# One core, convolution beside windowed attention: the positions of the convolution kernel laid out in three channel groups instead of two halves, with a new order of the first list

## The chip, the cores and the metric

The kernel runs on one core of one Trainium2 chip. The metric is the device time of one execution in microseconds (us). The kernel before was run three times: 361.35, 356.34 and 360.53 us, median 360.53. One execution was recorded by the hardware profiler; it took 360.97 us, and 359.0 us lie between its first and its last instruction (the span). Times in views of the profile count from the first instruction.

The engines are named as the profile names them: PE is TensorE, DVE is VectorE, ACT is ScalarE, POOL is GpSimd, SP is SyncE, which issues most of the DMA transfers; POOL issues the others.

## The reference

An input x of 2048 positions and 640 channels goes through two branches, and a gate mixes them. Branch A is attention with 32 heads over a window of eight positions with a step of two. Branch B is a long convolution of each channel: its kernel K is a sum over 192 complex exponentials, and the convolution is done by a Fourier transform of twice the length.

```python
g = _sigmoid((x * gate_w).sum(-1, keepdims=True))
a = _A_ref(x, A_wqkv, A_wo)
b = _B_ref(x, B_A_re, B_A_im, B_B_re, B_B_im, B_C_re, B_C_im, B_log_dt, B_Dskip)
return g * a + (1 - g) * b
...
P = jnp.exp(logdA[:, :, None] * l[None, None, :])
K = jnp.einsum("dn,dnl,dn->dl", Cc, P, dB).real
...
y = irfft2(Uf * Kf) + u * Dskip
```

## The kernel before

The work is written as tasks. A task has a name, an engine (or a choice of ACT and DVE) and a function that issues its instructions. Two lists of tasks are issued one after the other, each in an order written out by hand: SEQ1 for the first list (L62 on), SEQ2 for the second. In SEQ1 a number stands for a task in the order in which tasks are declared, and a letter A or D after it chooses the engine where there is a choice. Each engine runs its own tasks strictly in this order, so a task that waits holds up everything behind it on its engine; the waits between engines follow from the data and from buffers. Costs and due times that stand beside the tasks have no effect once the order is written out.

The first list holds:

- The parameters of the convolution kernel (names such as rs8, mk9, sp9): computed on DVE and ACT, stored to DRAM in twelve pieces (Sprm), and loaded as L tiles (L00, L01 and so on).
- The attention: transposes of x (turn, tev) into xT, projections (late, evicted by lev), products of queries and keys (prod on DVE, summed on PE by lg), softmax (max, neg, exp, sum, at), the weighted values (pv on DVE, gat on PE, oT) and the output product (wo on PE, ga on ACT or DVE). ast and asb send the weights through DRAM; vc loads a window of values.
- The kernel K in ten chunks of 8 x 2 channels for each of four groups of partitions: args on PE (arg), sines and exponentials on ACT (act), products on DVE (pq, three for each chunk), sums on PE (kmm), and an eviction (fin) into the tile E. A task of chunk c has c behind its letters: act90000 is the first sine of chunk 9.
- The expansion of K, twice, for five chunks each (a half): shift, own and other on DVE and move and near beside them lay out the tile X; xst stores X to DRAM (Kx) and xld loads it back in another order as the tile kc. X and kc are made with one tag, xkc, in a pool of one buffer, so the next X is written only when the last reader of the kc before it is done.
- The first step of the Fourier transform: f1 (ten transforms from the first half's kc), fk (ten from the second half's) and fu (twenty from the input, Usb, loaded by rows0 to rows7). Each is eight small matmuls on PE into one of two "ar" buffers and one cast of 128 x 1024 on ACT or DVE (f1e, fke, fue) into bufA or big. own of the second half is declared to come after the last f1.

The sines and exponentials live in rings in the tile big; a fifth slot for sines lies in bufA at column NXT = 10240, over xT, which is free by then. fu writes into big, and every fu comes after all pq.

The second list is the rest of the Fourier transform, the product with the transformed kernel, the transform back and the mixing. It starts when the first list's casts are done. Its order isn't touched.

Here own begins, with X in the shared buffer, and the load of kc takes the same tag:

```python
x = X["X"] = pool["kk"].tile([128, 8, 9, CH], BF16, name="X", tag="xkc")
...
half[hf, "kc"] = now["kk"].tile([128, 64, CH], BF16, name="kc", tag="xkc")
```

Of the kernel before, what the change touches and what calls it, by code (L numbers as in the profile page):

```python
# [11 lines left out]
ALU = mybir.AluOpType  # L12
AX = mybir.AxisListType
F32 = mybir.dt.float32
BF16 = mybir.dt.bfloat16
# [47 lines left out]
0 2 3 1 6 8 4 14 13 26 5 7 27 9 10D 11D 12 18 74 76 28 75A 77A 78 79A 82 80 83D 15 17 23 81A 114 115D 120 94 56 121D 19 20 21 88 116 95A 89A 117A 37 100 92 104 101A 29  # L63
105A 93A 22 24 34D 35D 31 36 39 42 108 109A 25 86 118 106 90 119A 102 107A 32 103A 87A 110 96 84 16 38 30 111A 135 45 97A 40 33 46 41 136A 98 99A 43 44 229 51D 52 47 53
60 62D 122 146 85A 123A 57 147A 91A 125 129 230 126A 61 63 112 48 130A 113A 50 231 59 64A 152 154 153A 65A 155A 67 139 222 232 66 233 49 58 69 54 140A 68 70 55 71 72 234
127 137 73 235 128A 236 143 237 138A 223 144A 516 238 133 265 239 131 134D 240 148 267 224 132A 241 242 150 225 149A 151A 226 243 266 269 517 244 563 562 245 518 520 268
141 270 519 521 271 522 524 272 523 273 994 124 221 145 228 264 156 525 274 526 528 167 275 301 168D 142A 527 529 276 530 532 531 533 178 534 536 180 535 537 179A 303 538
540 539 541 175 181D 246 176D 186 542 544 277 278 543 545 187A 279 182 546 548 302 304 157 554 305 307 547 183A 549 158A 159 184 160A 306 308 550 552 551 553 185D 309 337
173 280 609 281 608 227 177 188 310 564 566 171 311 174A 565 312 567 313 172A 161 314 568 570 162A 569 571 556 315 339 165 572 574 338 573 575 166D 341 555 340 576 577
578 342 169 343 345 579 170A 163 580 582 199 581 583 584 586 585 587 557 344 346 558 588 590 589 591 200A 249 164D 559 347 600 373 203 592 594 593 204A 595 348 210 211A  # L70
205 560 596 598 206D 375 561 349 597 207 208D 350 201 351 189 602 599 202A 190A 610 612 611 613 601 374 376 377 614 616 247 615 617 379 618 620 191 248A 619 621 622 624
378 380 197 623 192A 625 626 628 252 381 605 409 198A 627 629 603 604 630 631 632 606 633 634 635 382 636 216 212 411 383 607 637 213D 646 316 655 352 654 317 638 217A
639 640 384 250 642 641 385 251A 643 644 645 214 386 656 648 387 195 215A 657 658 660 647 253 410 412 196A 659 661 254A 701 700 388 662 664 663 665 193 194A 282 651 413
666 667 668 255 257 670 256D 218 669 671 672 673 649 674 675 285 258D 415 219D 676 677 650 678 679 414 680 681 682 259 683 684 686 685 687 652 688 689 692 417 416 209 300
690 418 702 691 703 704 261 705 260A 706 708 283 707 709 710 653 694 445 419 262A 288 711 712 693 714 713 715 284D 447 697 716 718 717 719 695 720 721 722 420 724 723 725
755 756 263 353 726 727 286 289 728 729 730 696 732 731 733 734 698 421 735 318 287D 290D 738 699 736 291 737 757 758 759 760 739 761 762 422 763 765 764 766 740 423 743
292D 741 767 768 801 802 769 446 448 742 771 293 770 773 772 775 774 776 777 744 778 294A 779 781 295 780 782 783 784 449 321 745 793 451 795 746 785 787 786 789 297 788
296A 790 791 803 792 804 805 450 806 807 794 809 808 811 298A 810 812 319 813 453 320A 814 815 796 816 817 818 452 819 820 821 454 823 822 824 825 826 798 749 324 455 481
827 828 322 456 829 797 830 831 832 457 325 747 748A 833 458 834 835 799 836 837 323D 483 839 326A 750 459 800 424 847 848 299 389 751 894 893 460 220 336 372 752 849 327
838 850 851 482 852 841 485 853 484 854 855 840 857 856 858 859 486 861 860 487 328D 489 862 842 863 329 331 865 844 330D 864 866 867 869 488 868 871 870 873 843 872 874  # L80
875 877 333 876 878 879 881 880 882 845 354 332D 885 846 887 883 884 895 897 490 896 899 898 901 886 900 903 902 905 355 334A 904 906 491 357 360 356D 890 907 908 909 910
753 940 335 939 425 888 911 912 913 915 914 916 492 917 918 919 920 358 361 921 889 923 922 359D 362D 390 924 925 891 927 926 929 363 928 930 941 942 943 365 931 364D 892
366D 933 945 944 946 932 947 367 949 948 493 368D 950 951 952 369 953 391 955 393 934 392D 396 936 954 956 370A 935 494 957 371 754 995 996 997 408 998 999 1000 444 1001
# [79 lines left out]
class Attn:  # L163
# [20 lines left out]
    def window(self, pl, cst, pa):  # L184
# [8 lines left out]
        for n in range(2 * NKT):  # L193
# [8 lines left out]
            def ev(en, hf=hf, kt=kt, b=b):  # L202
                evict(nc, en, self.xT[:, hf, kt, :], b["tx"][:].rearrange("p a b -> p (a b)"))
# [4 lines left out]
    def plan_gate(self, pl, cst, pa, g_sb, late):  # L208
# [3 lines left out]
        def logit(_):  # L212
            b["gz"] = gz = pa.tile([128, 2, 512], F32, name="ar")
            for i in range(16):
                for kt in range(NKT):
                    nc.tensor.matmul(gz[:, 0, i:i + 1], self.xT[:, i // 8, kt, (i % 8) * 128:(i % 8 + 1) * 128], self.gw[:, kt:kt + 1], start=(kt == 0), stop=(kt == NKT - 1))
# [1095 lines left out]
```

## Time and profile before

| | before |
|---|---|
| median of 3 runs | 360.53 us (356.34 to 361.35) |
| profiled execution | 360.97 us |
| its span | 359.0 us |
| mean granted PE clock | 0.961 |
| first list ends, second begins | 283.3 us |
| busy, share of the span | DVE 87%, ACT 84%, PE 82%, POOL 22% |

A line of the groups names the line of code, the engine and the operation, then the tile written and the tiles read (numbers of buffers left out), the shape, the count, and behind the bar the busy time in us and the mean of one in ns. A line of a timeline begins with the start and the duration in us; rows of equal instructions that follow each other are merged (x8), and in brackets stand the idle time of the engine before it and what ended that. SPq and POOLq are issue slots, not transfers. Casts that go through the helper `evict` carry its line (L470 on ACT, L472 on DVE); there the tile names tell which task it is. bp is the result of f1, fk and fu, tb that of projections and output products.

### The profile page before, as it was taken

What the parts mean: (1) busy time and instruction counts of PE and PEld (TensorE: products, weight loads), DVE (VectorE), ACT (ScalarE), POOL (GpSimd) and SP (SyncE); (2) the same over time, 40 slices, a digit from 0 to 9 for tenths busy, and PEclk for the clock granted to TensorE, in tenths of its full rate; (3) what the DMA queues carried; (4) which work ended last, traced back from release to release, by engine and by line L of the source; (5) the groups of instructions that cost most, each with busy time, mean ns of one, the idle gap of its engine ahead of it and who ended that gap; (6) DMA issues with size and microseconds to landing.
All of it is one profiled execution on the core that took longest, in us unless ns stands there. A gap on an engine that the chain in (4) does not pass through costs nothing. (4 is left out here: it accounts for less than half of the span.)

```text
span 359.0 us, 12203 instructions
## 1 busy us (share of the span) xinstructions
PE 293.7 (82%) x5271; PEld 173.4 (48%) x5286; DVE 311.5 (87%) x413; ACT 303.0 (84%) x417; POOL 78.3 (22%) x125
## 2 busy tenths in 40 slices
PE   0199999699999999888887869999997799978760
PEld 0065564234544545445443424566664556647650
DVE  2899999669999899999998987999993479999982
ACT  1699997578989999999997979999895599888881
POOL 8930090211020100100012122416010023310032
PEclk9999999989999999999998978999998899999995
DMA  7951289421501611461256867489653149943047
GB/s 259 370 175 57 82 213 268 120 66 19 150 11 27 122 40 19 140 129 30 71 109 192 190 152 137 95 177 256 172 153 101 38 126 225 228 95 75 4 98 199
DMA packets 44042, 46.60 MB, mean 130 GB/s; under 512 B 24517, under 2 KB 38133, under 8 KB 43733
## 3 DMA queue, kind: packets, MB, share of 16 engines
q1 hardware_dynamic: 36116, 24.43, 26.2%
q0 software_dynamic: 5840, 20.55, 22.5%
q10 hardware_dynamic: 2032, 0.85, 0.9%
q8 instruction: 41, 0.67, 0.8%
q14 instruction: 13, 0.10, 0.1%
HBM read 31.31 MB, written 14.51 MB: 128 GB/s over the span
## 5 line engine op out<-in xcount | busy, mean ns | idle before, releaser
L291 PE MATMUL tb<-bufA 128*128 128x512 bf16 x285 | 71.7, 387 | 2.8 <-issue 1.1
L748 PE MATMUL ar<-Rarg,L 64*128 64x304 bf16 (+1 forms) x480 | 55.3, 282 | 14.7 <-ACT big L760 5.9
L760 ACT ACTIVATE big<-ar 128x608 bf16<-128x608 int16 x96 | 59.0, 681 | 8.2 <-PE ar L748 5.7
L762 ACT ACTIVATE big<-ar 128x864 bf16<-128x864 f32 x60 | 50.3, 917 | 3.6 <-PE ar L748 3.3
L291 PEld LDWEIGHTS <-bufA 128*128 128x128 bf16 x300 | 33.2, 120 | 31.7 <-issue 9.3
L420 DVE TENSOR_TENSOR pv<-vc,asb 128x4096 bf16<-128x4096 bf16 (+1 forms) x24 | 46.3, 1928 | 1.4 <-PE tb L426 1.4
L748 PEld LDWEIGHTS <-L 64*128 64x128 bf16 x480 | 21.4, 94 | 48.8 <-issue 41.9
L1009 PEld LDWEIGHTS <-PHI 128*128 128x128 bf16 x288 | 26.8, 99 | 18.0 <-issue 8.4
L801 PE MATMUL kps<-qq,pt 128*32 128x22 bf16 (+1 forms) x2560 | 26.3, 175 | 4.2 <-issue 4.2
L444 PE MATMUL tb<-wo_sb,oT 128*128 128x320 bf16 x160 | 28.1, 311 | 0.0
L801 PEld LDWEIGHTS <-pt 128*32 128x32 bf16 (+1 forms) x2560 | 22.5, 91 | 11.6 <-issue 8.7
L351 DVE TENSOR_TENSOR prod<-qk 128x2048 bf16<-128x2048 bf16 x20 | 24.1, 1220 | 2.9 <-PE lg L357 2.8
L351 DVE TENSOR_TENSOR prod<-prj 128x2048 bf16<-128x2048 bf16 x20 | 24.0, 1219 | 0.6 <-PE lg L357 0.5
L345 POOL DMA_DIRECT2D vc<-vS x16 | 11.5, 725 | 57.1 <-DVE pv L420 54.0
L426 PE MATMUL tb<-pv,ind 128*64 128x512 bf16 (+1 forms) x192 | 22.4, 361 | 0.2
L785 DVE TENSOR_TENSOR qq<-big 128x1408 bf16<-128x1408 bf16 x24 | 21.2, 885 | 0.0
L470 ACT ACTIVATE bufA<-bp 128x1024 bf16<-128x1024 f32 x16 | 16.0, 1032 | 5.6 <-PE bp L1232 5.5
L1009 PE MATMUL fp<-big,PHI 128*128 128x320 bf16 x112 | 17.9, 304 | 3.0 <-ACT sp_u L470 3.0
L200 PE MATMUL ar<-ident,xn 128*128 128x128 bf16 x80 | 8.1, 263 | 15.0 <-DMA xn<-in_A_x_dram 14.3
L470 ACT ACTIVATE sp_u<-fp 128x1280 bf16<-128x1280 f32 x14 | 17.3, 1237 | 3.4 <-PE fp L1009 3.4
L470 ACT ACTIVATE prj<-tb 128x512 bf16<-128x512 f32 x28 | 17.1, 612 | 3.1 <-PE tb L291 3.0
L470 ACT ACTIVATE big<-bp 128x1024 bf16<-128x1024 f32 x19 | 18.6, 1023 | 1.0 <-PE bp L1232 0.8
(173 smaller groups left out, 587.2 us busy)
## 6 DMA issues: line engine op xcount, KB each, us to landing
vc<-vS POOLq DMA_DIRECT2D x16, 327.5 KB, 6.9
PHI<-c_phi POOLq DMA_DIRECT2D x8, 384.0 KB, 4.9
Sprm<-pc SPq DMA_DIRECT2D x12, 240.0 KB, 2.0
L<-Sprm SPq DMA_DIRECT2D x80, 36.0 KB, 2.6
xn<-in_A_x_dram SPq DMA_DIRECT2D x4, 640.0 KB
gaS<-ga SPq DMA_DIRECT2D x8, 320.0 KB, 3.0
Usb<-in_A_x_dram POOLq DMA_DIRECT2D x8, 320.0 KB, 5.0
gaF<-gaS SPq DMA_DIRECT2D x8, 320.0 KB, 7.3
```

The lines of the kernel that those rows point to most:

```text
L291: nc.tensor.matmul(ppf, self.wq[:, kt, which * D + e:(which + 1) * D:5], self.xT[:, c0 // 1024, kt, c0 % 1024:c0 % 1024 + SC], start=(kt = ...
L351: nc.vector.tensor_tensor(b[e][:], self.part(ch, 0)[:, e, o:o + C].unsqueeze(1).to_broadcast([128, W, C]), win(self.part(ch, 1)[:, e, :], ...
L420: nc.vector.tensor_tensor(b["pv", e][:, 0:2 * n], taps, aw, ALU.mult)
L426: nc.tensor.matmul(b["op", e][64 * a:64 * a + 64, 0:n, :], self.twin, b["pv", e][:, a:2 * n:2, w, :], start=(w == 0), stop=(w == HV - 1), ...
L444: nc.tensor.matmul(apf[:, :320], b["oT"][:, e, i * 128:(i + 1) * 128], wo_sb[:, e, hf * 320:(hf + 1) * 320], start=(e == 0), stop=(e == 4))
L470: nc.scalar.activation(o, i, ACT.Identity)
L748: nc.tensor.matmul(ar[:, g2, a0:a0 + ncol], L[rows, sb, gp, l0:l0 + 128], R[rows, c0:c0 + ncol], start=True, stop=True, tile_position=(64 ...
L760: nc.scalar.activation(dst[:, 2 * gp:2 * gp + 2, sub, :], ar[:].bitcast(I16)[:, :, 0:2 * SW:2], ACT.Sin, scale=SCL)
L762: nc.scalar.activation(dst[:, 2 * gp:2 * gp + 2].rearrange("p g s n -> p g (s n)"), ar[:, :, 0:2 * EW], ACT.Exp)
L785: nc.vector.tensor_tensor(qq[:], trg[:, :, KI:].rearrange("p a (v m) -> p a v m", v=2), exq[:, :, KI:].unsqueeze(2).to_broadcast([128, 32, ...
L801: nc.tensor.matmul(kps[32 * g:32 * g + 32, h, NM * ql:NM * ql + NM], pt[rows, k, v, :], qq[rows, k, v, :], start=(g not in started), stop= ...
L1009: nc.tensor.matmul(o.rearrange("p (c x) -> p c x", x=32), phis[fb][:, fl, kind, :], B[:, :, 2 * f1 + ri].rearrange("p c q g -> p c (q g)") ...
```

## The change

The ten chunks are expanded in three groups, of four, four and two chunks, instead of two halves of five. E, nxt, X and kc are made at the size of the largest group and used up to the width of the group at hand; there are three DRAM tensors Kx instead of one, and three times shift, move, near, own, other, xst and xld. f1 has sixteen transforms (f10 to f115, for groups 0 and 1) and fk four (fk16 to fk19, for group 2). own of a group comes after the transforms of the group before it.

The two halves of xT change places in bufA, and the ring's fifth sine slot moves to column 16384. A transform of the input (fu) now comes only after those pq that read the part of the ring that it overwrites, instead of after all pq. SEQ1 is a new order throughout, including the choice of ACT or DVE for many evictions. The Dskip values are loaded by twelve small DMAs instead of eight.

```diff
-NXT = 10240
+NXT = 16384
...
-HC = NCH // 2
-CH = 2 * HC * CQ
+GRP = ((0, 4), (4, 8), (8, 10))
+GC = 2 * CQ * max(b - a for a, b in GRP)
...
-        self.Kx = dr.tile([2, 8, 4, KI, 8 * CH], BF16, name="Kx")
-
-    def expand(self, hf, E, pool, psp, S12):
+        self.Kx = [dr.tile([8, 4, KI, 8 * 2 * CQ * (b - a)], BF16, name=f"Kx{a}") for a, b in GRP]
+
+    def expand(self, gi, E, pool, psp, S12):
...
+        g0, g1 = GRP[gi]
+        CH = 2 * CQ * (g1 - g0)
...
-            x = X["X"] = pool["kk"].tile([128, 8, 9, CH], BF16, name="X", tag="xkc")
+            x = X["X"] = pool["kk"].tile([128, 72 * GC], BF16, name="X", tag="xkc")[:, 0:72 * CH].rearrange("p (h s c) -> p h s c", h=8, s=9)
...
-            f = pl.add(f"fin{c}", "D", 0.46, fn, deps=[m] + ([half["cp"]] if c == HC else []), after=fins[-1:], rel=[("kb", m0)], due=due)
-            if cl == HC - 1:
-                expand(hf, f, due + (pr["xl"] if hf == 0 else -50.0))
+            f = pl.add(f"fin{c}", "D", 0.46, fn, deps=[m] + ([half["cp", gi - 1]] if c == g0 and gi else []), after=fins[-1:], rel=[("kb", m0)], due=due)
+            if c == g1 - 1:
+                expand(gi, f, due)
...
-            if name == "f1":
-                half["own"].after.append(m)
+            if gi is not None and gi + 1 < len(GRP):
+                half["own", gi + 1].after.append(m)
...
-        for n in range(2 * HC):
-            first("f1", lambda: half[0, "kc"], Bk, n, half[0, "ld"] + [cst], xdone, pr["f0"] + pr["f1"] * n)
+        for gi, (a, b) in enumerate(GRP):
+            for n in range(2 * (b - a)):
+                first("f1" if b < NCH else "fk", lambda gi=gi: half[gi, "kc"], Bk, n, half[gi, "ld"] + [cst], (kg.pqs if b == NCH else []) + xdone, pr["f0"] + pr["f1"] * n, c0=a, gi=gi)
...
         for n in range(2 * NCH):
-            first("fu", lambda: P["Usb"], None, n, ub + [cst], kg.pqs, pr["u0"] + pr["u1"] * n)
...
+            lo = 2048 * (n // 2)
+            first("fu", lambda: P["Usb"][:], None, n, ub + [cst], [kg.pqs[k] for a, b, k in ends if a < lo + 2048 and b > lo], pr["u0"] + pr["u1"] * n)
```

The stretch of the new order around own1 (own of group 1), by engine, from act90000 on:

```
ACT  act90000 act90001 act90010 act90011 act90100 f1e0 near1 act90101 act90110 act90111 oT44 act90200 act90201 ga400 act90210
     f1e3 f1e7 f1e4 ga401 f1e6 f1e5 ga410 f1e1 ga411 f1e2 act90211 oT50 fue1 fue2 oT54
PE   arg90000 kmm800 arg90001 gat40 gat42 arg90010 arg90011 kmm810 arg90100 f10 sum7 move1 arg90101 arg90110 kmm811 arg90111
     gat44 arg90200 arg90201 wo400 arg90210 f13 wo401 f17 f14 kmm820 f16 wo410 f15 wo411 f11 f12 gat50 kmm900 arg90211 gat52 fu1 fu0
DVE  pq81 oT40 pv44 pq82 oT42 own1 other1 pv50 pq90 fin8 pv52 pq91 pv54 at7 fue0 oT52 f1e12 pq92 pv60 ga500 ga501 pv62 ga510
     ga511 fin9 shift2 own2 oT60 pv64 other2 pv70 ga600 ga601 fue19 ga610 pv72 pv74 fue8 fke17 fke16 ga710 fke19 fke18
SP   xst1S xld1S gaS4 ast7 asb7 gaS5 xst2S xld2S gaS6 gaS7
POOL rows0 xld0G rows1 rows2 rows3 vc1280 rows4 rows5 vc1536 rows6 xst1G rows7 xld1G vc1792 xst2G phi2 gates2 gates0 gates3 phi0 xld2G
```

In the order before, own1 (of the second half) stands after fin9, and all ten f1 stand ahead of it between chunk 9's args and kmm911; ahead of xst0 on POOL stand vc0 and vc256 next to each other right after halo1, where the new order has vc0, lst12, gst, halo2, vc256.

More of the change, by code (lines that the diff above doesn't have):

```diff
@@ L841, in near @@
         def near(en):
[L842 removed]
+            nxt = X["nxt"] = pool["kk"].tile([128, 7 * GC], BF16, name="nxt")[:, 0:7 * CH].rearrange("p (m c) -> p m c", m=7)
             for pt, (b0, n) in enumerate(((0, 4), (4, 3))):
@@ L1165, in gated_mix_kernel @@
     at.window(pl, acst, pa)
-    Dk = keep.tile([128, 2, CH], BF16, name="Dk")
+    Dk = keep.tile([128, 2 * CQ * NCH], BF16, name="Dk")
     nc.gpsimd.memset(Dk[:], 0.0)
@@ L1205, in fetch @@
                 for g in (0, 1) if e == "S" else (2, 3):
-                    kx.load(hf, half[hf, "kc"], g, nc.sync if e == "S" else nc.gpsimd)
-            half[hf, "ld"] = [pl.add(f"xld{hf}{e}", e, d, fetch, deps=st, due=due, dma=1.7) for e, d in (("S", 1.4), ("G", 1.1))]
+                    kx.load(gi, half[gi, "kc"], g, nc.sync if e == "S" else nc.gpsimd)
+            half[gi, "ld"] = [pl.add(f"xld{gi}{e}", e, d, fetch, deps=st, due=due, dma=1.7 * n / 5) for e, d in (("S", 1.4), ("G", 1.1))]
```

127 lines of the change are left out of this document (63 added, 64 removed).

## The prediction

> **What bounds the kernel now.** I read the page first (parts 1 and 2), then the table of windows, then the timelines of the windows where an engine stands idle, and the groups of instructions for durations.
>
> ```profile
> span 359.0 us, 12203 instructions
> PE 293.7 (82%) x5271; PEld 173.4 (48%) x5286; DVE 311.5 (87%) x413; ACT 303.0 (84%) x417; POOL 78.3 (22%) x125
> ACT  1699997578989999999997979999895599888881
> ```
>
> ```profile
> core 0: us, PE busy (x) PEld busy (x) DVE busy (x) ACT busy (x) POOL busy (x), PEclk, DMA share, GB/s
> 200.00:220.00 20.00, 16.02 (x415) 7.49 (x414) 16.04 (x22) 16.58 (x27) 4.38 (x8) 0.83 0.79 174
> 220.00:240.00 20.00, 18.94 (x494) 11.05 (x497) 19.96 (x28) 19.84 (x30) 5.96 (x8) 1.00 0.61 129
> 240.00:257.00 17.00, 15.80 (x428) 11.47 (x421) 16.98 (x26) 15.81 (x20) 6.16 (x11) 1.00 0.75 187
> 257.00:283.30 26.30, 21.88 (x264) 14.47 (x261) 18.50 (x23) 20.32 (x24) 1.78 (x3) 0.93 0.40 130
> ```
>
> VectorE (DVE) and ScalarE (ACT) bound the first list together: from 220 to 257 DVE is idle for 0.06 us and ACT for 1.35. Whatever holds either of them there is paid in full. The one large hole is the end of the list, 257 to 283.3, where DVE is idle for 7.8 us and ACT for 6.0. The timelines say why:
>
> ```profile
> 253.84 0.52 DVE L1215 CAST E<-kps 128x352 bf16<-128x352 f32 x1
> 255.41 1.66 DVE L847 COPY X<-E 128x640 bf16<-128x640 bf16 x8
> 256.99 0.73 DVE L847 COPY X<-nxt 128x80 bf16<-128x80 bf16 x3
> 257.34 0.37 SPq L875 DMA_DIRECT2D Kx<-X  x1
> 264.07 1.45 SPq L881 DMA_DIRECT2D kc<-Kx  x2
> 272.78 1.24 PE L1232 MATMUL bp<-F1c,kc 64*128 64x128 bf16 x16 [2.37 <-DMA kc<-Kx]
> 274.06 1.22 DVE L472 CAST bufA<-bp 128x1024 bf16<-128x1024 f32 x1 [3.18 <-PE bp L1232]
> 281.84 1.23 DVE L472 CAST bufA<-bp 128x1024 bf16<-128x1024 f32 x1 [0.56 <-PE bp L1232]
> 283.30 2.03 PE L1009 MATMUL fp<-bufA,PHI 128*128 128x320 bf16 x7 [1.11 <-ACT bufA L470]
> ```
>
> After the last kernel chunk (fin9, 253.84) its half is laid out (own1, other1), stored to DRAM (issued at 257.34, landed by 264.07: 6.7 us), loaded back (264.07 to 272.78: 8.7 us), and then ten transforms and casts follow until the second list starts at 283.30. The second list is the same in both kernels; it keeps its 75.7 us (283.30 to 359.0). So the forecast is the place of that start.
>
> **The end of the list, by itself: a gain.** The last group has two chunks where the last half had five. The round trip took 15.4 us; of that I keep two fixed parts of 2.6 us (the median landing of the 36 KB loads below) and scale the other 10.2 by 2/5: 5.2 + 4.1 = 9.3 us, between 6.2 (all of it scales) and 15.4 (none does). Four casts instead of ten follow it.
>
> ```profile
> L<-Sprm SPq DMA_DIRECT2D x80, 36.0 KB, 2.6
> ```
>
> Alone, this would let DVE run through. Counted task by task, its list up to fin9 is about 3 us longer in the new order (work that moved ahead), so fin9 ends at 257.5, and 17.5 us of DVE work (shift2 to fke18, with the durations of the part after next) plus some 2 of waits would end the list near 277: 6 us less.
>
> **The new wait: own1.** X and kc share one buffer (tag xkc, one slot). The new order expands group 1 while group 0's columns still stand in that buffer, so own1 waits until all eight f1 transforms of group 0 have been read out of it. In the order of each engine own1 is the next DVE task after pq82 and oT42, while the eighth transform, f12, comes on PE behind arg90210, f13, f17, f14, f16, f15 and f11. Each transform needs one of two "ar" buffers, so f12 starts when ACT has done f1e5. That point is counted on ACT's list:
>
> ```profile
> 229.78 1.25 ACT L760 ACTIVATE big<-ar 128x608 bf16<-128x608 int16 x2
> 234.03 0.45 ACT L470 ACTIVATE oT<-tb 128x256 bf16<-128x256 f32 x1
> 235.49 0.55 ACT L453 ACTIVATE ga<-tb,g_sb 128x320 bf16<-128x320 f32 x1
> 240.13 4.89 ACT L470 ACTIVATE bufA<-bp 128x1024 bf16<-128x1024 f32 x5
> 255.59 0.71 ACT L470 ACTIVATE nxt<-nxp 128x320 bf16<-128x320 f32 x2
> 242.11 0.46 PE L1232 MATMUL bp<-F1c,kc 64*128 64x128 bf16 x8 [0.23 <-ACT bufA L470]
> ```
>
> From act90000 to f1e5 the new list has 11 sines of 0.60, six casts of 0.95, near1 (0.65), oT44 (0.38) and two ga (0.45): 6.6 + 5.7 + 0.65 + 0.38 + 0.9 = 14.2 us. (A record overlaps the next by about 0.08 us, so I take distances between starts: two sines make 1.25, five casts 4.89.) act90000 started at 229.78. Ahead of it the new list gives ACT three more oT and one more ga, one lev less and near0 less: +0.6. Against this stands a start that may be earlier:
>
> ```profile
> 22.61 33.77 SPq L614 DMA_DIRECT2D Sprm<-pc  x12
> 50.28 2.86 POOL L345 DMA_DIRECT2D vc<-vS  x4
> 63.78 4.23 SPq L721 DMA_DIRECT2D L<-Sprm  x8
> 65.66 0.77 PE L748 MATMUL ar<-Rarg,L 64*128 64x304 bf16 x4 [1.69 <-DMA L<-Sprm]
> 44.49 0.85 POOL L317 DMA_DIRECT2D vS<-pv  x1 [21.99 <-ACT pv L470]
> ```
>
> The last parameter store was issued by 56.4 and the loads that need it only at 63.78, with four window loads (vc0, vc256) in flight from 50.28; the new order puts vc256 behind lst12 and gst. PE's wait of 1.69 bounds the gain, zero is the other end; I take 1.5, since half of the competing bytes go. So act90000 starts at 228.9, f1e5 ends at 243.1, and with 0.46 for f12 own1 starts at **243.5**.
>
> DVE is there long before:
>
> ```profile
> 231.22 0.69 DVE L783 TENSOR_TENSOR pt<-big 128x1024 bf16<-128x1024 bf16 x1
> 231.82 0.69 DVE L784 TENSOR_TENSOR pt<-big 128x1024 bf16<-128x1024 bf16 x1
> 232.42 0.89 DVE L785 TENSOR_TENSOR qq<-big 128x1408 bf16<-128x1408 bf16 x1
> 233.22 0.55 DVE L391 RECIPROCAL rs<-lg 128x64 f32<-128x64 f32 x1
> 233.81 0.69 DVE L392 TENSOR_TENSOR at<-at,rs 128x512 bf16<-128x512 bf16 x1
> ```
>
> These are pq82 and at7 of before. DVE's work up to pq82 is 1 us shorter in the new order, but gat40 and gat42 are later on PE, so oT42 ends between 233 and 236: a hole of 8 to 10.5 us. Queued behind own1 on DVE are other1, pv50, pq90, fin8; for these wait gat50 and kmm900 on PE, next in PE's order after f12, and behind them arg90211 and so ACT, which has only f1e1, ga411 and f1e2 (2.4 us) until then. So ACT doesn't use the hole either.
>
> **What is left after own1.** Counted on the new DVE list from own1 on, with these durations less 0.08 each:
>
> ```profile
> L420 DVE TENSOR_TENSOR pv<-vc,asb 128x4096 bf16<-128x4096 bf16 x16 | 36.5, 2282 | 0.3 <-PE tb L426 0.3
> L455 DVE TENSOR_SCALAR ga<-tb,g_sb 128x320 bf16<-128x320 f32 x20 | 10.8, 546 | 1.9 <-PE tb L444 1.9
> L420 DVE TENSOR_TENSOR pv<-vc,asb 128x2048 bf16<-128x2048 bf16 x8 | 9.7, 1218 | 1.1 <-PE tb L426 1.1
> L472 DVE CAST oT<-tb 128x512 bf16<-128x512 f32 x10 | 6.9, 686 | 2.9 <-PE tb L426 2.7
> ```
>
> Six large pv at 2.20 (13.2), three small at 1.14 (3.4), three pq at 2.00 (6.0), eight casts of transforms at 1.15 (9.2), eight ga at 0.47 (3.7), two oT (1.2), two fin (0.9), at7 (1.2), own1 and other1 (2.0: 2.4 at width 80, 1.9 if it scales to 64), shift2, own2 and other2 (1.5: between 1.0 scaled and 2.6): 42.3 us. As a check, the kernel before had 32.0 us of DVE work left at 243.5 (13.5 of the window to 257, and 18.50). Waits: 1 us at f1e12 (group 1's columns come about 14 us after other1, at own1 + 16, and f112 is wanted at 15); 2.5 in the last four casts, which alternate with the last output products (the last seven DVE tasks of before held 3.0 us of waits from 274.06 to 283.07); 0.5 elsewhere; together 4, between 1.5 and 6. Group 2 isn't late: other2 ends at own1 + 28.6, its columns come at + 37.9, and DVE reaches them at about + 38.5. End of the list: 243.5 + 42.3 + 4 = 289.8, 6.5 us after 283.3.
>
> [...] PE stands behind own1 until pv50 is done (own1, other1, pv50: 4.2 us), an idle stretch that before does not have there. The trace has such a case: after the 2.37 us in front of 272.78 the granted clock was 0.50.
>
> ```profile
> 273.00:274.00 1.00, 1.00 (x17) 0.82 (x17) 0.00 (x0) 0.37 (x1) 0.00 (x0) 0.50 0.08 18
> ```
>
> [...]
>
> From the trace alone, a half clock in the 4 us after own1 costs between 0 (DVE has pq90 and pv52 to do) and 2; I take 0.5. The sum is then 360.97 (the profiled execution, 1.97 above its span) + 7.0 = **368.0**. The three runs have a median of 360.53, 0.4 less.
>
> **What costs nothing.** The number of casts stays 40. The halves of xT change places together with the ring's fifth sine slot, whose first writer waits for the same 30 projections. Four more tiny Dskip loads take 2 us of POOL ahead of 44.49, where it idles for 21.99. xld0 on POOL now waits behind rows0 for prod74, which belongs to the time of chunk 6, and f10 wants its columns only in that of chunk 9. ast7 and asb7 stand on SP behind xld1, which waits until about own1 + 8, but at7 is only done at + 13; vc1792 on POOL likewise; pv70 wants both at + 28.6. Starting the input's transform by region gives nothing here, as fu1 stands behind gat52, about own1 + 10 = 253.5; in the kernel before it began at 248.4.
>
> ```profile
> 248.37 1.20 PE L1232 MATMUL bp<-F1c,Usb 64*128 64x128 bf16 x16
> ```
>
> **The rivals.**
> - *The wait is covered* (other side). It decides if f12 is read by the time DVE arrives, about 235; for that ACT must be 8 us ahead of my count. Its idle time between 200 and 220 (3.4) and PE's 1.69 speak for some of it, its full slices before that against. Then the end gains 6: 355; with the 1.5 us of the start 353. Chance 0.12, of it 0.08 faster by over 2%.
> - *Half the hole*: ACT 4 to 5 us earlier, own1 at 239: 363. 0.13.
> - *The hole grows*: half clock paid in full (1.7), asb7 or group 1's columns late (2), ACT without the early start (1.5): 373. 0.25.
> - *The forecast*: 365 to 371. 0.50.
>
> **How the numbers follow.** Two per cent, about what a measurement of this kernel can tell from no change, is 7.2 us: 353.3 and 367.7. Of the forecast's 0.50 I put 0.35 above that line. Slower 0.35 + 0.25 = 0.60; within 0.15 + 0.13 + 0.04 = 0.32; faster 0.08. The range of 8 in 10 leaves out the first rival and the far end of the third: 361 to 375.
>
> **What would show it.** Right: a DVE gap of 8 to 11 us ahead of the first X<-E copy of group 1, released by PE, starting near 234; an ACT gap of some 5 us shortly after; the second list's first product near 290; the last kc load within 6 us of its issue. Wrong: that gap under 4 us; own1 before 239; or a hole in another place, such as DVE waiting for parameters or for asb7.

## The result, and the profile after

The changed kernel took 371.94 us (median of four runs, 369.55 to 374.65) against 360.73 for the kernel before (four runs on the same chip, 356.34 to 361.35): the ratio is 1.034, 95% interval 1.023 to 1.045, slower. The profiled execution took 372.19 us. The prediction was 368.0, with a range of 361 to 375.

The first lines of its page, as those shown of before: the span, the busy times and ACT's 40 slices. ACT drops to 6, 2 and 5 tenths in the 27th to 29th slice (240.8 to 268.5 us).

```profile
span 370.4 us, 12252 instructions
...
PE 294.9 (80%) x5274; PEld 173.3 (47%) x5290; DVE 312.7 (84%) x421; ACT 304.5 (82%) x423; POOL 89.7 (24%) x132
...
ACT  1699996978999999999996898962598489998880
```

The table of windows, columns as in the prediction. DVE, which had been busy for 19.96 of 20 us and 16.98 of 17 in the second and third window of before, now stands for 7.3 and 5.0 us there; PE's granted clock falls to 0.78.

```profile
220.00:240.00 20.00, 17.05 (x391) 9.85 (x389) 12.72 (x16) 17.47 (x28) 3.45 (x6) 0.91 0.50 111
240.00:257.00 17.00, 10.33 (x218) 5.95 (x212) 12.03 (x22) 8.42 (x13) 5.79 (x5) 0.78 0.44 126
257.00:283.30 26.30, 23.68 (x441) 15.79 (x436) 22.93 (x35) 19.74 (x25) 7.00 (x12) 0.82 0.51 137
```

The timelines of DVE, PE, ACT and SP say where, and what the second list waited for:

```profile
234.64 0.68 DVE L472 CAST oT<-tb 128x512 bf16<-128x512 f32 x1
244.97 1.46 DVE L849 COPY X<-E 128x512 bf16<-128x512 bf16 x8 [9.65 <-PE bp L1233]
...
244.48 0.45 PE L1233 MATMUL bp<-F1c,kc 64*128 64x128 bf16 x8 [0.25 <-ACT bufA L470]
249.25 1.84 PE L426 MATMUL tb<-pv,ind 128*64 128x512 bf16 x8 [4.31 <-DVE pv L420]
...
252.77 0.68 ACT L760 ACTIVATE bufA<-ar 128x608 bf16<-128x608 int16 x1 [5.68 <-PE ar L748]
...
246.68 0.38 SPq L877 DMA_DIRECT2D Kx<-X  x1
251.44 1.43 SPq L882 DMA_DIRECT2D kc<-Kx  x2
...
260.99 0.81 PE L1233 MATMUL bp<-F1c,kc 64*128 64x128 bf16 x8 [2.17 <-DMA kc<-Kx]
261.84 1.22 DVE L472 CAST bufA<-bp 128x1024 bf16<-128x1024 f32 x1 [1.94 <-PE bp L1233]
...
276.33 0.36 SPq L877 DMA_DIRECT2D Kx<-X  x1
280.14 1.44 SPq L882 DMA_DIRECT2D kc<-Kx  x2
...
287.56 0.46 PE L1233 MATMUL bp<-F1c,kc 64*128 64x128 bf16 x7 [1.01 <-DMA kc<-Kx]
288.06 1.23 DVE L472 CAST bufA<-bp 128x1024 bf16<-128x1024 f32 x1 [1.96 <-PE bp L1233]
...
295.37 1.25 PE L1010 MATMUL fp<-bufA,PHI 128*128 128x320 bf16 x8 [1.11 <-ACT big L470]
```

DVE ends oT42 at 235.3 and stands for 9.65 us, until PE has run f12 (244.48); then own1 goes. PE stands behind it for 4.31 us (gat50 needs pv50) and ACT for 5.68 (act90211). Group 1's columns take from 246.68 (store issued) to 260.99, group 2's from 276.33 to 287.56. The second list begins at 295.37, 12.1 us later than in the kernel before, and lasts 75.0 us (75.7 before).

Of the signs that the prediction names, the gap ahead of own1, the gap on ACT and the last load of kc (its pieces landed 5.6 us after their issue, median) came as forecast; the second list's first product came at 295.4 and not near 290.

Nearly all of the loss lies in the last stretch. From the first exponential of chunk 9 (act9100) to the second list's first product it is 60.2 us before and 72.1 after, and act9100 starts only 0.1 us later:

```profile
222.21 1.76 ACT L762 ACTIVATE big<-ar 128x864 bf16<-128x864 f32 x2
```

```profile
223.24 1.67 ACT L762 ACTIVATE big<-ar 128x864 bf16<-128x864 f32 x2 [1.75 <-PE ar L748]
```

The first row is of before: its second exponential, at 223.1, is act9100 (283.30 - 223.1 = 60.2); the other is of after (295.37 - 223.24 = 72.1). This distance, called the last stretch below, is the measure for the experiments, since what lies ahead of it wanders by some us from execution to execution (last section). In the table below the medians are of all executions, the ratios leave out those more than 1.5% above the fastest of their kernel, and as the profiled executions of `clock` and `clock_busy` are longer than the other runs of their kernels by a few us, only distances are used of them.

### The profile page after: what moved, and what is told of

Its sections match the earlier page's. It is cut to its first block, busy times and chain, and to the rows that moved or that the text cites. A ratio compares the mean times of both kernels' runs of the same rounds, so it can differ in the third digit from the quotient of the medians.

```text
span 370.4 us, 12252 instructions
## 1 busy us (share of the span) xinstructions
PE 294.9 (80%) x5274; PEld 173.3 (47%) x5290; DVE 312.7 (84%) x421; ACT 304.5 (82%) x423; POOL 89.7 (24%) x132
## 5 line engine op out<-in xcount | busy, mean ns | idle before, releaser
L762 ACT ACTIVATE big<-ar 128x864 bf16<-128x864 f32 x60 | 50.4, 921 | 6.4 <-PE ar L748 6.0
L801 PEld LDWEIGHTS <-pt 128*32 128x32 bf16 (+1 forms) x2560 | 23.3, 92 | 14.5 <-issue 10.4
L444 PE MATMUL tb<-wo_sb,oT 128*128 128x320 bf16 x160 | 29.8, 324 | 0.0
L426 PE MATMUL tb<-pv,ind 128*64 128x512 bf16 (+1 forms) x192 | 23.4, 374 | 5.6 <-DVE pv L420 5.6
L470 ACT ACTIVATE big<-bp 128x1024 bf16<-128x1024 f32 x17 | 17.2, 1027 | 6.3 <-PE bp L1233 6.3
L470 ACT ACTIVATE sp_k<-fp 128x1280 bf16<-128x1280 f32 x14 | 17.3, 1237 | 3.9 <-PE fp L1010 3.5
L1010 PE MATMUL fp<-bufA,PHI 128*128 128x320 bf16 x112 | 17.5, 298 | 3.6 <-ACT sp_k L470 2.1
L760 ACT ACTIVATE bufA<-ar 128x608 bf16<-128x608 int16 x24 | 14.9, 679 | 6.5 <-PE ar L748 6.5
L200 PE MATMUL ar<-ident,xn 128*128 128x128 bf16 x80 | 8.1, 264 | 14.9 <-DMA xn<-in_A_x_dram 14.1
L783 DVE TENSOR_TENSOR pt<-big 128x1024 bf16<-128x1024 bf16 x24 | 16.5, 686 | 2.9 <-issue 2.6
```

The costliest lines, as they stand in the source:

```text
L426: nc.tensor.matmul(b["op", e][64 * a:64 * a + 64, 0:n, :], self.twin, b["pv", e][:, a:2 * n:2, w, :], start=(w == 0), stop=(w == HV - 1), ...
L444: nc.tensor.matmul(apf[:, :320], b["oT"][:, e, i * 128:(i + 1) * 128], wo_sb[:, e, hf * 320:(hf + 1) * 320], start=(e == 0), stop=(e == 4))
L470: nc.scalar.activation(o, i, ACT.Identity)
L760: nc.scalar.activation(dst[:, 2 * gp:2 * gp + 2, sub, :], ar[:].bitcast(I16)[:, :, 0:2 * SW:2], ACT.Sin, scale=SCL)
L762: nc.scalar.activation(dst[:, 2 * gp:2 * gp + 2].rearrange("p g s n -> p g (s n)"), ar[:, :, 0:2 * EW], ACT.Exp)
L801: nc.tensor.matmul(kps[32 * g:32 * g + 32, h, NM * ql:NM * ql + NM], pt[rows, k, v, :], qq[rows, k, v, :], start=(g not in started), stop= ...
```

## The experiments

Ratios are to the kernel before, run beside them on the same chip. Each edit is made to the changed kernel, unless another is named.

| run | median us | ratio, 95% interval | last stretch us |
|---|---|---|---|
| (before) | | | 60.2 |
| (after) | 371.94 | 1.034, 1.023 to 1.045 | 72.1 |
| own_tile | 363.75 | 1.009, 1.005 to 1.013 | 63.8 |
| f1_first | 366.20 | 1.012, 1.005 to 1.019 | 66.4 |
| own_buffer | 366.06 | 1.013, 1.002 to 1.025 | 68.1 |
| fill | 369.55 | 1.026, 1.018 to 1.034 | 70.8 |
| clock | 369.49 | 1.023, 1.013 to 1.034 | 73.4 |
| clock_busy | 371.45 | 1.028, 1.021 to 1.035 | 73.3 |
| vc256_early | 374.61 | 1.038, 1.028 to 1.047 | 71.8 |
| reordered | 367.32 | 1.020, 1.014 to 1.026 | 64.6 |
| order_only | 370.10 | 1.028, 1.018 to 1.038 | 73.5 |
| phi_late | 365.85 | 1.025, 1.013 to 1.037 | 71.0 |
| late_order | 370.93 | 1.034, 1.024 to 1.043 | 72.9 |
| filled | 370.22 | 1.036, 1.024 to 1.047 | 70.3 |

How far two runs can be told apart, `clock` shows: it is the changed kernel's own program once more (see there), and it has a ratio of 1.023 instead of 1.034 and a last stretch of 73.4 us instead of 72.1. clock_busy and vc256_early, whose orders are the same from chunk 9 on, have 73.3 and 71.8. Differences of up to about 1.6 us in the last stretch, or 0.01 in the ratio, say nothing.

### The shared buffer: own_buffer, own_tile

own_buffer lays group 1's X out in bufA.

```diff
-            x = X["X"] = pool["kk"].tile([128, 72 * GC], BF16, name="X", tag="xkc")[:, 0:72 * CH].rearrange("p (h s c) -> p h s c", h=8, s=9)
+            xt = self.bufA[:, 2048 * g0:2048 * g0 + 72 * CH] if gi == 1 else pool["kk"].tile([128, 72 * GC], BF16, name="X", tag="xkc")[:, 0:72 * CH]
+            x = X["X"] = xt.rearrange("p (h s c) -> p h s c", h=8, s=9)
...
+    kx.bufA = P["bufA"]
```

> The changed kernel, but group 1's X is laid out in a stretch of bufA that is still free (columns 8192 to 12799) instead of in the buffer that it shares with kc; nothing else is moved. Theory (the shared buffer's wait, with what follows from it, is the loss): the DVE gap ahead of group 1's first X<-E copy falls from 9.65 us to under 1.5, that copy starts at 235 to 237 instead of 245.0, its store, load and transforms move up with it, and the second list starts at 283 to 287 instead of 295.4: 359 to 363 us. Rival A (the queues, not the buffer: PE's f12 stands ahead of gat50 and kmm900 and still ends near 244.5, so DVE's time is only spent waiting a few tasks later, for pv52 to pv54): a new DVE gap of over 5 us between 240 and 250, second list at 290 or later, 366 to 371. Rival B (the loss lies elsewhere in the order): gap gone, but 369 or more.

Its gap ahead of own1 is gone, but two waits came with the place. The timelines of SP, POOL and ACT of this kernel:

```profile
238.13 0.62 SPq L879 DMA_DIRECT2D Kx<-bufA  x1
...
238.40 0.65 POOL L876 DMA_DIRECT2D Kx<-bufA  x1 [3.59 <-ACT bufA L470]
...
243.09 1.02 ACT L470 ACTIVATE bufA<-bp 128x1024 bf16<-128x1024 f32 x1 [4.57 <-DMA Kx<-bufA]
```

bufA is also what the casts of group 0 write, into other columns. The stores of X waited for such casts (3.59) and the next cast for the stores (4.57): the waits are set as if the stretches touched. So the last stretch became only 4.0 us shorter, the time of 366.06 misses the 359 to 363 of the theory, and the run does not price the shared buffer. own_tile takes a tile that nothing else uses at that time:

```diff
+            xt = self.qk if gi == 1 else pool["kk"].tile([128, 72 * GC], BF16, name="X", tag="xkc")
+            x = X["X"] = xt[:, 0:72 * CH].rearrange("p (h s c) -> p h s c", h=8, s=9)
...
     kx = KExpand(ctx, tc, Dk)
+    kx.qk = at.qk[0]
```

> The changed kernel, but group 1's X is laid out in the query and key tile, which nothing reads any more after the fifth window's products; kc of group 1 still goes into the buffer that kc of group 0 stands in. Theory (the shared buffer's wait is the loss, in two parts: own1 waits for f12, and so do the loads of kc): the DVE gap of 9.65 us ahead of own1 is gone (under 1.5), own1 starts some 5 us after act90000 instead of 14, its stores land before f12, the loads go out right after f12 and f112 starts 9 to 11 us after f12 instead of 16.5; DVE waits 3 to 5 us there. The second list starts 6 to 9 us earlier counted from act90000: 363 to 366 us, ratio 1.005 to 1.02. Rival (DVE's gap only moves, to fue0 and f1e12): sum of DVE waits from oT42 on as large as before, under 3 us gained, ratio 1.025 or more.

Its timelines of DVE, SP and PE:

```profile
232.77 0.68 DVE L472 CAST oT<-tb 128x512 bf16<-128x512 f32 x1
233.37 1.74 DVE L849 COPY qk<-E 128x512 bf16<-128x512 bf16 x8
...
253.37 1.22 DVE L472 CAST bufA<-bp 128x1024 bf16<-128x1024 f32 x1 [3.73 <-PE bp L1235]
...
235.36 0.38 SPq L878 DMA_DIRECT2D Kx<-qk  x1
243.23 1.43 SPq L883 DMA_DIRECT2D kc<-Kx  x2
...
242.72 0.48 PE L1235 MATMUL bp<-F1c,kc 64*128 64x128 bf16 x8 [0.25 <-ACT bufA L470]
252.43 0.90 PE L1235 MATMUL bp<-F1c,kc 64*128 64x128 bf16 x8 [3.32 <-DMA kc<-Kx]
```

own1 follows oT42 without a gap, 4.6 us after act90000; the stores go out at 235.36, the loads right after f12 (242.72), and f112 starts 9.7 us after f12 (16.5 in the changed kernel). The last stretch is 8.3 us shorter and the ratio falls from 1.034 to 1.009: the theory's numbers, and not the rival's. The wait for the buffer was worth 8.3 of the 11.9 us by these two executions; by the ratios it is 1.4% (against `clock`) to 2.5%, 5 to 9 us. DVE's sums over the stretch from act90000 to the second list say what the other 3.6 are. One row each of the table of windows (third figure: DVE busy), for before, after and own_tile:

```profile
229.78:283.30 53.52, 47.50 (x912) 31.77 (x901) 45.67 (x62) 46.21 (x60) 10.91 (x19) 0.96 0.61 160
```

```profile
230.56:295.37 64.81, 51.41 (x973) 33.26 (x970) 47.97 (x71) 45.51 (x64) 15.27 (x21) 0.87 0.49 132
```

```profile
228.76:285.89 57.13, 48.55 (x975) 32.53 (x970) 48.05 (x71) 45.60 (x64) 14.56 (x22) 0.94 0.59 155
```

DVE idles for 7.85, 16.84 and 9.08 us. Taking the wait away gives back 7.8 us of idle time; against the kernel before own_tile has 2.4 us more DVE work and 1.2 us more idle time in it. (Over the whole span the changed kernel has only 1.2 us more DVE work, 312.7 against 311.5, so about half of the 2.4 was moved into this stretch by the order.) So in this order, and even without the wait, the short last group does not make the list shorter.

### The order of the transforms: f1_first

The buffer stays shared; group 0's eight transforms and casts, move1 and near1 go ahead of act90000 in SEQ1.

```diff
-ACT  ... act9121 exp7 act90000 act90001 act90010 act90011 act90100 f1e0 near1 ... act90210 f1e3 f1e7 f1e4 ga401 f1e6 f1e5 ga410 f1e1 ga411 f1e2
+ACT  ... act9121 f1e0 f1e3 f1e7 f1e4 f1e6 f1e5 f1e1 f1e2 near1 exp7 act90000 act90001 ... act90210 ga401 ga410 ga411
-PE   ... wo311 arg90000 kmm800 ... arg90210 f13 wo401 f17 f14 kmm820 f16 wo410 f15 wo411 f11 f12 gat50
+PE   ... wo311 f10 kmm800 f13 f17 gat40 f14 f16 gat42 f15 f11 kmm810 f12 move1 arg90000 ... wo401 kmm820 wo410 wo411 gat50
```

> The changed kernel with the buffer still shared, but the eight transforms of group 0 (f10 to f12, their casts, move1 and near1) put ahead of act90000 instead of among and behind the last sines; all other tasks keep their order. Theory (own1 waits because these transforms come late, not because there is one buffer): f12 and own1 start together within 6 us after oT40, the gap ahead of own1 falls under 1.5 us, group 1's columns come 8 to 9 us earlier; new waits of 2 to 4 us where pq90 needs kmm811, which now stands behind more sines; second list 6 to 9 us earlier: 363 to 366, ratio 1.005 to 1.02. Rival (work only changes places: the sines come 8 us later and DVE waits for them instead): waits of over 6 us at pq90 or fin8, ratio 1.025 or more.

The DVE timeline:

```profile
234.74 1.54 DVE L849 COPY X<-E 128x512 bf16<-128x512 bf16 x8
...
242.10 0.69 DVE L783 TENSOR_TENSOR pt<-big 128x1024 bf16<-128x1024 bf16 x1 [3.06 <-ACT big L760]
...
247.73 0.52 DVE L1216 CAST E<-kps 128x352 bf16<-128x352 f32 x1 [3.54 <-PE kps L801]
```

With one shared buffer own1 starts at 234.74 without a gap, so it is the late transforms that make the buffer cost. Two new waits take 6.6 us of the 9.65 back in DVE's time: 3.06 at pq90, which the profile puts down to the later sines, within the 2 to 4 expected there, and 3.54 at fin8, behind kmm820, which the expectation didn't have. Together they are as long as the rival's 6, but the ratio of 1.012 is the theory's; the last stretch is 5.8 us shorter, about the 6 to 9.

### DVE's gap or own1's chain: fill

```diff
-DVE  ... oT42 own1 other1 pv50 pq90 fin8 pv52 pq91 ...
+DVE  ... oT42 pv50 pq90 pv52 own1 other1 fin8 pq91 ...
```

> The changed kernel with pv50, pq90 and pv52 put ahead of own1 on DVE, so that 6.4 of the 9.65 us of the gap hold work; the buffer is still shared. If idle DVE time is what costs: 6.4 us less, 365 to 366. If own1's lateness costs through its chain (store, load and transforms of group 1, 16 us from own1 to its columns): the gap falls to about 3 us, own1 stays near 245, and the wait for group 1's first columns grows from 1.9 us to 6 to 8, so the time stays at 369 to 372.

The timelines of DVE and PE:

```profile
242.87 1.47 DVE L849 COPY X<-E 128x512 bf16<-128x512 bf16 x8 [3.33 <-PE bp L1233]
...
252.94 1.09 PE L1233 MATMUL bp<-F1c,Usb 64*128 64x128 bf16 x15 [5.46 <-DMA Usb<-in_A_x_dram]
254.06 1.22 DVE L472 CAST big<-bp 128x1024 bf16<-128x1024 f32 x1 [4.40 <-PE bp L1233]
...
258.87 1.23 DVE L472 CAST bufA<-bp 128x1024 bf16<-128x1024 f32 x1 [2.99 <-PE bp L1233]
```

The gap fell from 9.65 to 3.33 as the work put into it says, and of these 6.3 us 4.40 came back at fue0 and 1.05 more at f1e12; the last stretch is 1.3 us shorter, no more than a repeat differs. So it is not DVE's idle time as such that costs but own1 as the head of a chain. The place of the new wait was not the expected one: most of it is at fue0, not at f1e12. The row of PE says why: the input's transform waited 5.46 us for the last rows of the input. Their load (rows7) stands on POOL behind xst1G, the store of own1's X. So own1 holds up the input too.

### PE's half clock: clock, clock_busy

PE's clock in the changed kernel was 0.50 from about 249.4 to 266. Both runs add 36 products of constants at the head of gat50. In `clock` their condition asks for the loop's variable sc, which has run to 7 when the products are issued, so none of them is in the program, and the run is a repeat of the changed kernel. clock_busy hands sc over:

```diff
-                def gather(_, e=e, n=n, b=b):
+                def gather(_, e=e, n=n, b=b, sc=sc):
                     b["op", e] = ps.tile([128, 2, C], F32, name="tb", bufs=2)
+                    if sc == 5 and e == 0:
+                        for _ in range(36):
+                            nc.tensor.matmul(b["op", e][:].rearrange("p a b -> p (a b)")[:, 0:256], self.ident, self.wo_sb[:, 0, 0:256], start=True, stop=True, skip_group_check=True)
```

> The changed kernel with 36 further products (128x256, about 4 us, into gat50's own output tile, which its real products then overwrite) at the head of gat50, so that PE is busy while it would wait for pv50. Theory (the half clock from 249.4 to 266.4 follows from that idle stretch and costs 2 to 3 us of the list's end): the granted clock stays above 0.9 from 246 to 266 and the time falls to 368 to 370. Rival (the half clock lies beside DVE's work and costs nothing): the clock stays up and the time stays within 0.7 of 371.9. Rival (the clock falls from light load, whatever stood before): it falls again by 255.

> The changed kernel with 36 further products (128x256 of two constant tiles, into gat50's own output tile, which its real products then overwrite) at the head of gat50, so that PE works for about 4 us after f12 while it would wait for pv50. Theory (the half clock that starts near 249 follows from that idle stretch, and costs 2 to 3 us of the list's end): the granted clock stays at 1.00 for at least 10 us after f12, own1 to the second list's first sine or copy on ACT takes 49 us or less instead of 51.7, ratio 1.02 to 1.03. Rival (the half clock lies beside DVE's work): the clock stays up and that stretch stays within 0.7 us of 51.7. Rival (it follows from the light load that comes after): the clock falls within 8 us of f12 all the same.

As a repeat, `clock` has a gap of 9.65 us ahead of own1, as the changed kernel, and 51.7 us from own1 to the second list (50.4 there). The timeline and windows of clock_busy:

```profile
247.99 4.09 PE L426 MATMUL tb<-wo_sb,ident 128*128 128x256 bf16 x36
252.35 1.05 PE L429 MATMUL tb<-pv,ind 128*64 128x512 bf16 x8 [0.27 <-DVE pv L420]
254.79 0.65 PE L804 MATMUL kps<-qq,pt 128*32 128x22 bf16 x64 [1.39 <-DVE E L1219]
```

```profile
252.40:256.90 4.50, 1.90 (x74) 1.11 (x73) 4.50 (x6) 1.15 (x2) 3.83 (x4) 1.00 0.58 165
257.50:270.00 12.50, 9.20 (x143) 5.57 (x140) 10.24 (x13) 5.04 (x6) 1.48 (x2) 0.51 0.73 174
```

gat50 now took 1.05 us instead of 1.84, but kmm900 waited 1.39 for DVE (0.60 in the changed kernel). From own1 to the second list's first product it was 50.9 us, against 50.4 of the changed kernel and 51.7 of its repeat, and not the 49 or less of the theory: the half clock up to 257 lies beside DVE's work and costs nothing that stands out of the 1.3 us by which the two repeats differ. From about 257.5 the clock fell all the same (0.51 in the last row), 10 us after f12, so what the half clock costs behind that point was not tried.

### The start: vc256_early

```diff
-POOL ... halo1 vc0 lst12 gst halo2 vc256 lst22 ...
+POOL ... halo1 vc0 vc256 lst12 gst halo2 lst22 ...
```

> The changed kernel with window load vc256 put back directly behind vc0, ahead of lst12 and gst, where the kernel before has it. If its place gave the earlier start: act00000 goes from 65.9 back to 67 to 68. If that start is carried to the end: 373 to 374; if DVE's wait for asb0 at pv00 (2.73 us at 76.9) takes it up: 371 to 372.

The first sine in the changed kernel, then in this one:

```profile
65.95 2.46 ACT L760 ACTIVATE big<-ar 128x608 bf16<-128x608 int16 x4
```

```profile
68.31 1.25 ACT L760 ACTIVATE big<-ar 128x608 bf16<-128x608 int16 x2
```

It starts 2.4 us later, though the loads of L were issued a little earlier (58.40 against 59.09): the place of vc256 did give the earlier start. Whether it reaches the end (1.038 against 1.034) can't be told from these runs.

### Other orders: reordered, order_only, phi_late, late_order, filled

These tried for a version that beats both kernels, with longer reorderings from chunk 9 on. In short form:

```diff
 reordered, late_order, filled: X of groups 1 and 2 in self.qk, and for group 2
+now["kk"].tile([128, 64 * CH], BF16, name="kc2")
 reordered    PE  ... f10 gat40 gat42 f12 f14 gat44 f11 arg90000 wo400 ...      DVE ... own1 pq81 other1 ...
 order_only   ACT ... f1e1 f1e2 f1e7 f1e6 f1e3 f1e5 near1 ... act90000 ... fue1 ga500 act90211 ...   DVE ... pq92 f1e13 pv62 fin9 pv64 shift2 own2 ...
 phi_late     as order_only, POOL ... rows7 vc1536 xld1G vc1792 xst2G phi2 gates2 gates0 gates3 phi0 xld2G gates1 phi1
 late_order   as the changed kernel up to act90101, then pq92 ahead of f1e12, fin9 ahead of ga511
 filled       as late_order, POOL and SP as in the changed kernel, DVE ... pq92 oT52 fin9 pv60 pv62 f1e12 f1e15 ga500 shift2 own2 ...
```

> The three groups kept, X of groups 1 and 2 in the query and key tile, kc of group 2 in a buffer of its own (4 KB a partition, which is free), and the order of the list from chunk 9 on worked out anew: transforms of group 0 early, pq90 to pq92 and fin9 ahead of the output products, 25 casts between ACT and DVE changed over. If the three groups are worth the 6 us that the short tail promises once no buffer holds them up: second list at 278 to 283, 354 to 359 us, ratio 0.98 to 0.995. If the groups themselves cost (more transfers, more instructions) or the round trip can't be hidden: 361 or more, ratio 1.0 or above.

> The changed kernel with its own buffers (X and kc share one), only another order from chunk 9 on: the eight transforms of group 0 ahead of own1 and of the sines, kmm811 and kmm820 ahead of most sines, pq92 and fin9 ahead of the sixth window's output work, 29 casts between ACT and DVE changed over. Theory (the loss is the order around the shared buffer, not the three groups): no DVE gap over 1.5 us ahead of own1 or own2, second list at 280 to 284, 355 to 360 us, ratio 0.985 to 1.0. Rival (three groups cost more than the short tail gives, whatever the order): 362 or more, ratio 1.005 or above. Rival (PE stands still for 2 us and more within its own stream here too, as it did near 243 in the version reordered before): such a stretch ahead of wo4 or gat5 and a second list at 285 or later.

> The version with only another order from chunk 9 on, but with the spectra's tables (phi0 to phi2, 0.4 MB each) and the gate loads on POOL behind group 2's store again, where the changed kernel has them; there ACT waited 10.04 us for the store of the fifth window's output (issued at 244.0, in flight with the loads of kc, vc1792, rows7 and two of these tables). Theory (that store lands late because of the transfers beside it): it lands 4 to 8 us earlier, ACT's wait ahead of ga500 falls to 2 to 6 us, and the time falls by as much: 362 to 366, ratio 1.005 to 1.015. Rival (the tables have no part in it; the store waits behind kc, vc and rows): the wait stays above 8.5 us and the ratio at 1.025 or more.

> The version with X of groups 1 and 2 in the query and key tile and kc of group 2 in a buffer of its own, with the order of the changed kernel kept up to act90101 and another one only from there: pq92 and fin9 ahead of f1e12 and the sixth window's output work, so that DVE has work while group 1's columns come, and group 2's round trip starts some 6 us earlier; 22 casts changed over. Theory (what the version with its own tile still lacks to the kernel before is the wait for group 1's columns, 3.7 us, and for group 2's, some 2): second list 5 to 9 us earlier than there counted from act90000 (52 to 55 us from act90000 to the second list's first copy instead of 58.4), 355 to 360 us, ratio 0.985 to 1.0. Rival (ACT has no work to put there and the waits only change engines): 362 or more.

> X of groups 1 and 2 in the query and key tile, kc of group 2 in a buffer of its own, POOL's and SP's lists as in the changed kernel; the other engines in another order from act90101 on: pq92, fin9, pv60 and pv62 ahead of f1e12, the sixth window's output (ga500) only behind group 1's first casts, 17 casts between ACT and DVE changed over. Theory (the version with its own tile lacks the 3.7 us of the wait for group 1's columns and some 2 at group 2's; and the later ga500 keeps clear of its late store): 52 to 55 us from act90000 to the second list's first copy on ACT instead of 58.4, 356 to 361 us, ratio 0.985 to 1.0. Rival (what is moved ahead is given back at another wait): 58 us and more, ratio 1.007 or above.

None came near the 0.985 to 1.0 hoped for; apart from phi_late, which lies between its theory and its rival, all came out as their rivals say. In order_only own1 has no gap ahead of it (it starts at 230.1), and ACT stands at ga500 instead, which takes the tile ga that the store of the fifth window's output still reads. SP's and ACT's timelines, order_only first, then phi_late:

```profile
244.00 0.36 SPq L464 DMA_DIRECT2D gaS<-ga  x1
...
258.94 0.53 ACT L453 ACTIVATE ga<-tb,g_sb 128x320 bf16<-128x320 f32 x1 [10.04 <-DMA gaS<-ga]
```

```profile
241.59 0.36 SPq L464 DMA_DIRECT2D gaS<-ga  x1
...
254.41 0.53 ACT L453 ACTIVATE ga<-tb,g_sb 128x320 bf16<-128x320 f32 x1 [7.92 <-DMA gaS<-ga]
```

That store took 14.9 us, with the loads of kc, a window of values, rows and two tables in flight; without the tables 12.8, and the wait fell by 2.1 us. That is less than the 4 expected at least: the tables can be a part of it; what makes up the rest, the run does not show. late_order waits at the same place (6.69). In reordered and filled it is PE itself (last section).

## Why the prediction was right

- **The new wait** was as forecast, in place and size: a gap of 9.65 us (8 to 10.5), released by PE, followed by an ACT gap of 5.68 (about 5), because f12 stands behind f1e5. own_tile and f1_first take it away in two ways, with 8.3 and 5.8 us. own1 started at 244.97, 1.5 later than forecast: act90000 came at 230.56 instead of 228.9. The early start was there (65.95 instead of 67.7, and vc256's place gives it), but ACT lost it again at waits that the forecast didn't have, among them 3.36 us at 204.40 and 1.75 ahead of act9100, both behind a stop of PE (last section).
- **What is left after own1** was too small. Forecast were 42.3 us of DVE work and 4 of waits; the row for that stretch shows 43.20 and 7.24:

```profile
244.96:295.40 50.44, 38.59 (x651) 25.05 (x652) 43.20 (x64) 31.25 (x41) 12.79 (x17) 0.83 0.50 141
```

  The waits are f1e12 (1.94, forecast 1), the last casts (1.96, 0.96 and 0.51, together 3.4, forecast 2.5) and small ones elsewhere (0.27 and 0.64 at two output tasks among them, forecast 0.5 in all). The forecast read 3.0 us of waits out of the end of the kernel before; its rows there (0.28, 0.77, 0.63, 0.25 and 0.56) give 2.5. Group 2's columns were at own1 + 42.6 instead of + 37.9: other2 ended 2.9 later than counted, and the way through DRAM took 1.8 longer. With own1 1.5 later this makes the list's end 295.4 instead of 289.8, and with the shorter second list a time of 372.2 instead of 368.0.
- **"Alone a gain of 6 us"** is the step that failed, and the first rival's price with it: own_tile is the case in which the wait is covered, and it gave 363.75, ratio 1.009, not 353. That the sum of 368.0 is good all the same is not owed to this step, as the sum counts from own1 on. The step let DVE run through up to fin9, 27.7 us after act90000, with 19.5 us left behind it. In own_tile fin9 ended 35.1 us after act90000, with 29.8 of work and 5.3 of waits, and 22.0 us followed, with 18.2 of work and 3.8 of waits. The largest part is the waits ahead of fin9, which the step put at nothing: f1e12 stands ahead of fin9 in DVE's list and needs group 1's columns (3.73 of the 5.3 us). Work ahead of fin9 was 2.3 us more than counted, and the waits behind it 1.8 more than the 2. The way through DRAM is not much shorter for a smaller group: from the first store to the transform that waits for its columns five chunks took 15.4 us in the kernel before, four took 14.3 in the changed kernel (246.68 to 260.99), and two took 11.2 instead of the 9.3 assumed. In own_tile four took 17.1 (235.36 to 252.43). There the loads went out at 243.23, as f12 ended (243.2); how much of these 17.1 the shared buffer holds, that run does not show.
- **The other rivals**: half the hole did not come. The time lies above the 365 to 371 that got the chance of 0.50, and near the price of the larger hole (373), but of its three reasons none held as stated: the early start was there, though act90000 came 1.7 us late for another reason; the half clock showed no price up to 257; and group 1's columns came at own1 + 16.0, as forecast. The profiled execution is 4.2 us above the forecast: own1 came 1.5 us late and the work and the waits behind it were 4.1 us longer, while the 0.5 of the half clock and 0.7 of the second list were not needed. That the time falls on this rival's price is luck.
- **The half clock** was put at 0.5 us for the 4 us after own1; it lasted for about 17 (249.4 to 266.4), without a price that can be seen in the part tried. The 1.7 us for it in the sum of 373 is shown by no run: from own1 to the second list it was 50.9 us in clock_busy, where the clock stayed at 1.00 up to 256.9, against 50.4 in the changed kernel and 51.7 in its repeat.
- **What costs nothing**: the input's transform began at 255.73 and gave nothing, as forecast; no wait of DVE for asb7 or vc1792 shows.

## What to carry to other kernels

A single buffer that a later stage shares is paid for when its last reader comes late (9.65 us of DVE's time here): look up that reader in its engine's order before a stage is moved ahead of it, and move the reader too, or give the stage a tile that stands empty (one which no other engine is writing: in bufA, which ACT's casts also write, the waits were 3.59 and 4.57 us). Filling the gap in front of a late task gains little when the task heads a chain of transfers (in `fill` 6.3 us of the gap went, and the last stretch became 1.3 us shorter); the chain's head has to move. Count what stands in front of the shortened end, too: here group 1's casts stood ahead of fin9. And the way through DRAM, cut into smaller pieces, kept most of its length here (15.4 us for five chunks, 11.2 for two).

## What the runs showed of the hardware

PE stood still inside a block of products, with nothing in the profile that it waited for ("issue"). In the changed kernel it is a block of chunk 6's sums, at 203.80; in filled another at 255.13:

```profile
203.80 0.26 PE L801 MATMUL kps<-qq,pt 64*32 64x22 bf16 x14 [3.29 <-issue]
```

```profile
255.13 0.67 PE L1235 MATMUL bp<-F1c,Usb 64*128 64x128 bf16 x8 [3.54 <-issue]
```

```profile
253.00:255.00 2.00, 0.00 (x0) 0.00 (x0) 0.00 (x0) 0.00 (x0) 0.00 (x0) 0.83 1.15 285
```

In the last row, of filled, no engine is busy at all for 2 us, at a DMA share of 1.15. The first of these stops lies in a block of 64 products (kmm611; the block of 64 ahead of it takes 0.65 us). This block is in all thirteen profiled versions of the changed kernel, and the tasks ahead of it are the same in all but vc256_early; it took 4.08 us in the changed kernel, 4.10 in clock_busy, 3.55 in `clock`, 3.53 in reordered, and 1.58 in own_tile, 1.06 in phi_late, 0.87 in f1_first. So one and the same block took 0.87 to 4.10 us, and reordered and filled lost part of what they were meant to gain to such a stop (2.06 near 243; 3.54 and 1.92 near 255 and 259). PE's timelines of the fourteen profiles, from 60 to 300 us, have 30 such stops of over 0.6 us, and 27 of them lie in blocks of kmm, where 64 short products and their weight loads pass in 0.65 us. The page lists a DMA queue for instructions (packets, MB, share):

```profile
q8 instruction: 41, 0.67, 0.8%
```

The changed kernel has 41 of these packets, of 16 KB each, and 10,564 products and weight loads on PE, 258 for each packet. Counted over PE's records, the stops at 192.23, 203.80 and 222.19 of the changed kernel lie 512 and 768 records apart, those at 190.22 and 209.82 of the kernel before 768, and those at 255.13 and 258.86 of filled 256. And in the changed kernel and the kernel before PE goes on 1.3 to 1.6 us after a packet of this queue has ended, each of the five times. What PE waited for is not shown: no run varied it.

The granted clock fell in clock_busy, too, from 1.00 (252.40 to 256.90) to 0.51 (257.50 to 270.00), after 4.5 us in which PE was busy for 1.90 and never stood for over 1.4 us; and in the changed kernel it stayed at 0.50 for 16.5 us with PE busy for 12.37 of them:

```profile
249.50:266.00 16.50, 12.37 (x217) 6.81 (x214) 14.53 (x18) 5.59 (x8) 5.10 (x6) 0.50 0.72 181
```
